# Late units of a gated-recurrence and SwiGLU kernel: packing transfers on another queue, a 16-bit step in the weight decoding, another order inside transposes, and decayed k turned without TensorE

## The chip, the cores and the metric

The kernel runs on one core of one Trainium2 chip. The metric is the device time in microseconds (us) of one execution. Three timed executions of the kernel before gave a median of 611.0 us (610.39 to 611.38). One further execution was profiled; all profile lines come from it.

## The reference

The first half is a linear recurrence with a gate, for 4 batches, 8 heads, 768 tokens and 48 dimensions per head. The second half is a feed-forward block with 384 model and 1536 hidden dimensions on all 3072 tokens.

```
f = sigmoid(f_logit)
for t in range(S):
    state = f[t][:, None] * state + outer(k[t], v[t])      # per batch and head, 48 x 48
    y[t] = q[t] @ state
x = y as (B*S, H*D)
out = (silu(x @ w_gate) * (x @ w_val)) @ w_out
```

q, k, v and f_logit are 32-bit floats. The three weight matrices arrive as 64-bit floats, so the kernel has to make 32-bit floats of them itself.

## The kernel before, in words

**Units and chunks.** Tokens are cut into six chunks of 128 (`c` = 0 to 5). A unit `u` is one batch `b` of one chunk, numbered chunk by chunk: u = 4c + b, 24 units in all. One run of the generator `attention(u)` (L529) is one unit. It yields between its steps, and these steps are placed between other work. Two heads share one 128-partition tile (64 partitions each, 48 of them used), so a unit has four such pairs of heads (`HP` = 4).

**The steps of a unit.** Sigmoid of f; f, k and q transposed so that tokens lie along the free dimension; a backward scan of the gates into `tail` (L576), whose first column `whole` is the decay over the entire chunk; k multiplied with `tail` (L584, "decayed k", tile `kT`); a forward scan into `gate` (L598); q multiplied with `gate` (L604, tile `qT`); scores `sc` on TensorE (L617) and their masking into `A` on VectorE (L631); the old state times `whole` (`decay`, L537); the output `y` on TensorE; the update `dS` of the state (L697), which needs decayed k with tokens on the partitions again (`kt`); the new state (L706). ScalarE copies `whole` into a column of `least` (L623), which is checked once near the end.

**Two routes for the transposes.** Units of chunks 0 and 1 transpose f, k and q on TensorE. Units of chunks 2 to 5 (`c >= SQUARES`) transpose on VectorE: f, k and q are loaded into three single rooms (`rooms`, L398) such that VectorE's transpose of 32 x 32 squares gives the wanted layout (L565, L572, L601). Token t of a chunk has four residues i = t mod 4; each square holds one residue, so its transpose writes with a step of four elements. The f, k and q of the next unit are loaded (`load_after`, L709) once q has been transposed.

**kt.** In units 0 to 13 TensorE transposes decayed k (four instructions, L621) into PSUM and ScalarE copies it out (L629). In units 14 to 19 (`turned`, L586) VectorE transposes squares of decayed k into the room of the coming `qT` (`beside`, L591), four DMAs on SP's queue write it to a DRAM tile `turn` (L594), and one DMA on SP's queue reads it back as `kt` (L627). The last chunk needs no kt.

**From y to the block.** For batches 0 to 2 of a chunk, ScalarE copies `y` from PSUM into `yT` (L660) and ten DMAs on SP's queue pack it into `xT[c]` (L667). For batch 3, `decay` also builds a tile `diagonal`: GpSimd clears it (L544), two ScalarE copies fill it (L546), TensorE uses it for y (L677), and ScalarE copies y straight into `xT[c]`. `yT` and `diagonal` are the same buffer (tag "x", one buffer), so clearing `diagonal` of batch 3 waits until the packing DMAs of batch 2 have read `yT`.

**The feed-forward block.** Chunk 0 is computed plainly (`mlp_plain`). Chunks 1 to 5 use `mlp_fifteen`: fifteen products in place of eighteen for gate and val, four times, and then seven products in place of eight for the way down (`down_seven`, L1033), in the order one, six, two, three, four, five, seven. After "two", ScalarE copies the PSUM tile out (L1082), after which product "four" may use that bank again. While chunk c is in its block, units of chunk c+1 run beside it. Results go out by DMA (L800, L1065).

**Weights.** Each weight piece is fetched, ScalarE makes two 32-bit words from the two halves of each 64-bit number (`sizes`, L458: `up` and `top`), and VectorE joins them (`join`, L466): a clamp (L469), a shift and mask (L471), the two top bits of the number put on with `scalar_tensor_tensor` (L473, one instruction for each of `b // parts` slices), and an exact addition (L475).

**What sets the order.** `in_order` (L724) chains the instructions of each engine, SP and GpSimd among them, in the order in which they were traced. In the late part (from L1253) that order comes from a list of due times written by hand (`SCORES`, `CHAINS`, L828 to L842) against a clock that counts TensorE's work. So an instruction that waits holds up everything traced after it on its engine.

Of the kernel before, what the change touches and what calls it, by code (L numbers as in the profile page):

```python
# [9 lines left out]
FP32 = mybir.dt.float32  # L10
I32 = mybir.dt.int32
U32 = mybir.dt.uint32
AF = mybir.ActivationFunctionType
ALU = mybir.AluOpType

# [274 lines left out]
def short_path(ctx, tc, ident, least, judge, q, k, v, f_logit, moe_w_gate, moe_w_val, moe_w_out, out):  # L290
# [9 lines left out]
    nc = tc.nc  # L300
    B, H, S, D = q.shape
    C = 128
    NCH = S // C
    HP = H // 2
# [6 lines left out]
    N1 = C + 1  # L311
# [3 lines left out]
    SQUARES = 2  # L315
# [47 lines left out]
    def pairs(t, off=0):  # L363
        return t[:, off:off + HP * N1].rearrange("p (a t) -> p a t", t=N1)
# [30 lines left out]
    NI = C // Q  # L395
    RUN = NI * D

    rooms = {}  # L398
# [6 lines left out]
    def v_of(u):  # L405
        return vs[u % (NV if units[u][1] < SQUARES else NV // 2)]

    def squares(nm):
        return rooms[nm][:, Q:Q + HP * RUN].rearrange("t (a i e) -> t a i e", a=HP, i=NI)[:, :, :, 0:Q]

    def in_turn(t):

        return t.rearrange("p a (t i) -> p a i t", i=NI)

    def load(u, what="fkqv"):
        b, c = units[u]
        rows = slice(c * C, (c + 1) * C)
        for nm, src in (("f", f_logit), ("k", k), ("q", q), ("v", v)):
            if nm not in what:
                continue  # L420
            if nm == "v":
                dst = v_of(u)
            elif c < SQUARES:
                dst = raw[nm][u % NRAW]
            else:
                for n in range(4):
                    at = Q * (1 - n % 2)
                    nc.sync.dma_start(
                        out=rooms[nm][Q * n:Q * (n + 1), at:at + HP * RUN].rearrange("t (a e) -> t a e", a=HP),
                        in_=src[b, n // 2::2, rows, :].rearrange("a (t i) d -> t a (i d)", i=NI))  # L430
                continue
            nc.sync.dma_start(out=dst[:, :, 0:D], in_=src[b, :, rows, :].rearrange("h t d -> t h d"))

    def weight_piece(dst, src, parts):

        b, a, n = dst.shape[1:]  # L440
        if src.dtype == FP32:
            by_row = src.rearrange("p a (b n) -> p a b n", n=n)
            return (lambda: [nc.sync.dma_start(out=dst[:, :, i], in_=by_row[:, i]) for i in range(a)]), [], []
        shape = [128, b // parts, a, n]
        kept = {}

        def fetch():
            kept["w"] = wst.tile([128, a, 2 * b * n], I32, tag="w64", name="w64", bufs=4)
            nc.sync.dma_start(out=kept["w"], in_=src)

        def part(m):
            return slice(m * b // parts, (m + 1) * b // parts)

        def halves(m):
            words = kept["w"].rearrange("p a (b n two) -> p a b n two", two=2, n=n)[:, :, part(m)].rearrange("p a b n two -> p b a n two")
            return words[:, :, :, :, 0], words[:, :, :, :, 1]

        def sizes(m):  # L458
            lo, hi = halves(m)
            up = wst.tile(shape, I32, tag="up", name="up", bufs=NPART)  # L460
            nc.scalar.activation(up, lo.bitcast(U32), AF.Copy, scale=2.0 ** -29)
            top = wst.tile(shape, I32, tag="top", name="top", bufs=NPART)
            nc.scalar.activation(top.bitcast(FP32), hi.bitcast(FP32), AF.Abs)
            kept["up", m], kept["top", m] = up, top

        def join(m):  # L466
            lo, hi = halves(m)
            up, top = kept["up", m], kept["top", m]
            nc.vector.tensor_scalar(top.bitcast(FP32), top.bitcast(FP32), as_float(0x38000000), as_float(0x47F00000),  # L469
                                    op0=ALU.max, op1=ALU.min)  # L470
            nc.vector.tensor_scalar(top, top, 3, 0x3FFFFFFF, op0=ALU.logical_shift_left, op1=ALU.bitwise_and)  # L471
            for i in range(b // parts):
                nc.vector.scalar_tensor_tensor(top[:, i], hi[:, i], -(1 << 30), top[:, i], op0=ALU.bitwise_and,  # L473
                                               op1=ALU.bitwise_or)
# [35 lines left out]
    xT = {}  # L510
# [18 lines left out]
    def attention(u):  # L529
        b, c = units[u]  # L530
        fr, kr, qr = (raw[nm][u % NRAW] for nm in "fkq")
        v_ = v_of(u)
        gate, tail = (x[u % NROT if c < SQUARES else 0] for x in (gates, tails))

        diagonal = None

        def decay():  # L537
            nonlocal diagonal
            if c:
                nc.vector.tensor_tensor(decayed[:, :, 0:D], states[b], whole.broadcast_to((128, HP, D)), ALU.mult)  # L540
            if c and b == B - 1:

                diagonal = att.tile([128, HP, 2 * D], FP32, tag="x", name="diagonal")
                nc.gpsimd.memset(diagonal, 0.0)  # L544
                for par in range(2):
                    nc.scalar.copy(diagonal[rows_of(par), :, par * D:(par + 1) * D], decayed[rows_of(par), :, 0:D])  # L546
# [13 lines left out]
        else:  # L560
            p = transposed("fTp", fr)
# [22 lines left out]
        nc.vector.tensor_tensor(kT, kp, pairs(tail, 2)[:, :, 0:C], ALU.mult)  # L584
        yield
        turned = (SQUARES + 1) * B + 1 < u < (NCH - 1) * B  # L586
        if turned:


            beside = qT.rearrange("p a t -> p (a t)").rearrange("p (i m) -> p i m", i=NI)  # L590
            nc.vector.transpose(beside.rearrange("p i (a e) -> p a i e", e=Q), kT.rearrange("p a (i e) -> p a i e", e=Q))  # L591
            turn = turn_pool.tile([Q, NI, HP, NI, Q], FP32, tag="turn", name="turn")
            for r in range(NI):
                nc.sync.dma_start(out=turn[:, :, :, r, :].rearrange("t i a e -> t (i a) e"),  # L594
                                  in_=beside[Q * r:Q * (r + 1)].rearrange("t i (a e) -> t (i a) e", e=Q))
        yield

        nc.vector.tensor_tensor_scan(gate[:, 0:n], gate[:, 0:n], start, 1.0, op0=ALU.mult, op1=ALU.add)  # L598
        yield
        if c >= SQUARES:  # L600
            nc.vector.transpose(in_turn(qT), squares("q"))  # L601
            load_after(u)
        yield
        nc.vector.tensor_tensor(qT, qp, pairs(gate)[:, :, 1:N1], ALU.mult)  # L604
        nc.gpsimd.memset(pairs(gate)[:, :, 0:1], 0.0)
        if 0 < c < SQUARES:
            load_after(u)
# [6 lines left out]
        for a in range(HP):  # L614
            for par in range(2):
                r = rows_of(par)
                nc.tensor.matmul(sc[par][:, a * C:(a + 1) * C], lhsT=kT[r, a, :], rhs=qT[r, a, :], start=True, stop=True)  # L617
        if c < NCH - 1 and not turned:
            p = bank("kt")
            for a in range(HP):  # L620
                nc.tensor.transpose(p[:, a * C:(a + 1) * C], kT[:, a, :], ident)  # L621
        yield
        nc.scalar.copy(least[:, u, :], whole.rearrange("p a t -> p (a t)"))  # L623
        if c < NCH - 1:
            kt = att.tile([128, HP * C], FP32, tag="kt", name="kt")
            if turned:
# [13 lines left out]
        if c and b < B - 1:  # L640
# [17 lines left out]
            yT = att.tile([128, 2, HP // 2 * C], FP32, tag="x", name="yT")  # L658
            for par in range(2):
                nc.scalar.copy(yT[:, par, :], y[par][:, 0:HP // 2 * C])  # L660
            for h in range(H):
                a, par = h // 2, h % 2
                f = h * D
                while f < (h + 1) * D:
                    n = min((h + 1) * D, (f // 128 + 1) * 128) - f
                    r = W * (a % 2) + f - h * D
                    nc.sync.dma_start(out=xT[c][f % 128:f % 128 + n, f // 128, b * C:(b + 1) * C],  # L667
                                      in_=yT[r:r + n, par, a // 2 * C:(a // 2 + 1) * C])
                    f += n
        else:  # L670

# [22 lines left out]
        if c < NCH - 1:  # L694
            p = bank("dS")
# [129 lines left out]
    whole = NJ * TRIPLE + 7 * DOWN  # L825
# [82 lines left out]
    def lag(f, *args):  # L908
        lagging.append(lambda: f(*args))  # L909
# [123 lines left out]
    def down_seven(c, h):  # L1033
# [7 lines left out]
        kept = {}  # L1041
# [321 lines left out]
```

## Time and profile before

| | |
|---|---|
| median of three executions | 611.0 us |
| the profiled execution | 611.44 us |
| its span, first to last instruction | 609.6 us |
| TensorE matmuls busy | 595.8 us |
| VectorE busy | 494.3 us |
| ScalarE busy | 288.5 us |
| GpSimd busy | 7.6 us, 52 instructions |
| DMA issues on SP's queue for packing (L667) | 150 |
| DMA issues on SP's queue for kt by way of DRAM (L594, L627) | 24 + 6 |

In a line of instruction groups the columns are: line, engine, operation, output and input tiles, shapes, count, then busy us in all, mean ns of one, and the idle time just before them with what ended it. In a timeline they are: start, duration (both us from the start of the span), engine, line, operation, tiles, count, and in brackets the idle time before and what ended it. SPq is SP's queue. Matmul ends are modelled, so starts are the safer reading.

### The profile page before, as it was taken

The numbers are of one execution on the slowest core, as the hardware profiler recorded it, in microseconds if no ns is written. First come the engines' busy times: TensorE is split into PE (matmuls) and PEld (weight loads), VectorE is DVE, ScalarE is ACT, GpSimd is POOL, SyncE is SP. The second block draws the span as 40 slices with busy tenths as digits, with TensorE's granted clock in tenths as the row PEclk, the third lists the DMA queues.
The fourth block names the chain that finished last, engine by engine and source line by source line (L and its number), as shares of the span: only waits on it lengthen the run. The fifth ranks groups of instructions, "written<-read, shape, count | busy, mean of one in ns | idle before, by whom it ended". The sixth has DMA issues, their size and how long they took to land.

```text
span 609.6 us, 10796 instructions
## 1 busy us (share of the span) xinstructions
PE 595.8 (98%) x4036; PEld 491.1 (81%) x4036; DVE 494.3 (81%) x833; ACT 288.5 (47%) x554; POOL 7.6 (1%) x52
## 2 busy tenths in 40 slices
PE   7899999999999999999999999999999999999996
PEld 5744545667888799888899988899988899988896
DVE  7999989868999985999996789996878981566731
ACT  3466644313776522476732366742276730366600
POOL 1000000000000000000000000000000000000000
PEclk9999999999999999999999999999999999999999
DMA  9988372005312044323236334145313100100001
GB/s 199 260 194 295 126 247 79 5 15 159 95 39 70 23 108 115 105 53 96 61 89 145 94 97 110 35 112 120 110 44 90 27 6 10 53 1 1 0 1 59
DMA packets 109142, 54.10 MB, mean 89 GB/s; under 512 B 68760, under 2 KB 102168, under 8 KB 109080
## 3 DMA queue, kind: packets, MB, share of 16 engines
q1 hardware_dynamic: 107064, 50.56, 31.3%
q10 hardware_dynamic: 2016, 2.75, 1.2%
q8 instruction: 34, 0.56, 0.4%
q14 instruction: 28, 0.23, 0.1%
HBM read 44.04 MB, written 6.29 MB: 83 GB/s over the span
## 4 chain that ended last, share of the span: by engine, by line
PE 85%; DVE 10%; SPq 1%; issue 1%; DMA 1%; ACT 1%; POOL 0%; DVEq 0%; ACTq 0%; POOLq 0%
PE o L1056 17%; PE A L957 15%; PE B L957 12%; PE gate L755 5%; PE val L755 5%; PE o L957 5%; PE c L957 5%; PE sc L617 4%; PE o L778 3%; PE o L1119 3%; PE y L677 2%; PE y L656 2%; PE dS L697 2%; PE y L652 1%; DVE c L861 1%
## 5 line engine op out<-in xcount | busy, mean ns | idle before, releaser
L1056 PE MATMUL o<-w_out,h 128*128 128x192 f32 x360 | 62.0, 327 | 0.5 <-DVE h L909 0.5
L957 PE MATMUL A<-xs,w_both 128*128 128x256 f32 x240 | 62.1, 381 | 0.0
L1056 PEld LDWEIGHTS o<-w_out,h 128*128 128x128 f32 x360 | 58.7, 190 | 1.7 <-DVE h L909 0.8
L962 ACT COPY c<-A 128x512 f32<-128x512 f32 x40 | 23.3, 583 | 62.6 <-PE A L957 62.6
L962 ACT COPY aside<-A 128x512 f32<-128x512 f32 x60 | 35.1, 584 | 32.6 <-PE A L957 32.6
L858 DVE TENSOR_TENSOR c<-c,aside 128x512 f32<-128x512 f32 x60 | 41.6, 694 | 10.5 <-ACT aside L962 9.0
L957 PEld LDWEIGHTS A<-xs,w_both 128*128 128x128 f32 x240 | 44.9, 190 | 6.5
L909 DVE TENSOR_TENSOR h<-h,c 128x256 f32<-128x256 f32 x100 | 41.1, 419 | 7.3 <-ACT h L973 7.3
L861 DVE TENSOR_TENSOR c<-c,aside 128x512 f32<-128x512 f32 x60 | 41.4, 689 | 2.5 <-ACT aside L962 2.5
L973 ACT ACTIVATE h<-c 128x256 f32<-128x256 f32 x100 | 39.2, 416 | 8.4 <-DVE c L858 5.8
L1056 PE MATMUL o<-ws,h 128*128 128x192 f32 x240 | 41.5, 328 | 0.2 <-DVE A L631 0.2
L957 PE MATMUL B<-xs,w_both 128*128 128x256 f32 x160 | 41.2, 380 | 0.6 <-ACT aside L962 0.6
L957 PE MATMUL c<-xT,w_both 128*128 128x256 f32 x160 | 41.2, 380 | 0.5 <-DVE c L861 0.5
L957 PE MATMUL A<-xs,extra 128*128 128x256 f32 x160 | 41.2, 380 | 0.0
L957 PE MATMUL B<-xT,extra 128*128 128x256 f32 x160 | 41.1, 379 | 0.0
L962 ACT COPY aside<-B 128x512 f32<-128x512 f32 x60 | 35.1, 584 | 11.7 <-PE B L957 7.2
L631 DVE TENSOR_TENSOR A<-sc,causal 128x512 f32<-128x512 f32 x48 | 30.8, 684 | 11.3 <-PE sc L617 11.3
L1056 PEld LDWEIGHTS o<-ws,h 128*128 128x128 f32 x240 | 39.1, 190 | 0.8 <-DVE A L631 0.4
L861 DVE TENSOR_TENSOR c<-o,c 128x512 f32<-128x512 f32 x40 | 27.6, 690 | 10.0 <-ACT h L973 5.8
L957 PEld LDWEIGHTS c<-xT,w_both 128*128 128x128 f32 x160 | 30.3, 190 | 5.0 <-DVE c L861 0.9
L957 PEld LDWEIGHTS B<-xs,w_both 128*128 128x128 f32 x160 | 30.2, 190 | 5.0 <-ACT aside L962 1.0
L957 PEld LDWEIGHTS A<-xs,extra 128*128 128x128 f32 x160 | 30.3, 190 | 4.5 <-ACT c L962 0.4
(138 smaller groups left out, 1140.2 us busy)
## 6 DMA issues: line engine op xcount, KB each, us to landing
fsquares<-in_f_logit_dram SPq DMA_DIRECT2D x64, 96.0 KB, 2.6
ksquares<-in_k_dram SPq DMA_DIRECT2D x64, 96.0 KB, 2.3
qsquares<-in_q_dram SPq DMA_DIRECT2D x64, 96.0 KB, 2.2
v<-in_v_dram SPq DMA_DIRECT2D x24, 192.0 KB, 3.0
w<-in_moe_w_gate_dram SPq DMA_DIRECT2D x6, 768.0 KB, 6.3
w<-in_moe_w_val_dram SPq DMA_DIRECT2D x6, 768.0 KB, 5.1
w<-in_moe_w_out_dram SPq DMA_DIRECT2D x6, 768.0 KB, 5.3
out_dram<-ob ACTq DMA_DIRECT2D x14, 192.0 KB, 2.7
```

The lines of the kernel that those rows point to most:

```text
L617: nc.tensor.matmul(sc[par][:, a * C:(a + 1) * C], lhsT=kT[r, a, :], rhs=qT[r, a, :], start=True, stop=True)
L631: nc.vector.tensor_tensor(A[:, par], sc[par].rearrange("p (a t) -> p a t", t=C), causal.unsqueeze(1).broadcast_to((128, HP, C)), ALU.mult)
L755: nc.tensor.matmul(p, lhsT=w[:, j, i, :], rhs=xT[c][:, i, :], start=(i == 0), stop=(i == KT - 1))
L778: nc.tensor.matmul(p, lhsT=hidden_tile(h, n // 2)[:, n % 2 * 2 + b // 2, b % 2 * C:(b % 2 + 1) * C], rhs=w_out[:, j, :], start=(n == 0), s ...
L858: nc.vector.tensor_tensor(dst, a, b, ALU.add)
L861: nc.vector.tensor_tensor(dst, a, b, ALU.subtract)
L909: lagging.append(lambda: f(*args))
L957: nc.tensor.matmul(p[name][:, n, :], lhsT=weights_of[a][:, n, j, :], rhs=tokens[b], start=fresh and n == 0, stop=True, skip_group_check=True)
L962: nc.scalar.copy(t, p[name])
L973: nc.scalar.activation(dst, src[:, 0, :], AF.Silu)
L1056: nc.tensor.matmul(p[:, n, :], lhsT=lhsTs[j][:, n * C:(n + 1) * C], rhs=rhs[:, j, :], start=first and j == order[0] and n == 0, stop=j == ...
L1119: nc.tensor.matmul(p, lhsT=hidden_tile(h, j)[:, 2, n * C:(n + 1) * C], rhs=b22[:, j, :], start=j == order[0], stop=j == order[-1])
```

## The change

- **Packing.** For chunks 2 to 5 the packing DMAs (L667, 120 of the 150) go to GpSimd's queue, and so do the two output DMAs of L1065 in every chunk but the last.
- **16-bit ops for the top bits.** ScalarE writes `up` as 16-bit numbers into the low half of each 32-bit word. VectorE then puts the two top bits into the high half, by one 16-bit instruction per piece that reads every fourth 16-bit number of the source and writes every second one. The `scalar_tensor_tensor` of L473 goes.
- **Pairs in transposes.** For k and q of chunks 2 to 5 the transpose writes with a step of two elements (two residues side by side, the other two in another half of the tile). The multiplication that follows (`multiply`) reads its operand in that order. k's transpose now goes to the room of `qT`, and q's to the room of `tail`; since that overwrites `whole`, the copy to `least` on ScalarE comes before the forward scan, and `whole` is read from `least` afterwards.
- **Decayed k by VectorE and DRAM.** `turned` holds for all twelve units of chunks 2 to 4 (u = 8 to 19), and `beside` lies in k's room.
- **Loads.** For chunks 2 to 5 q is loaded ahead of k.

```
-        for nm, src in (("f", f_logit), ("k", k), ("q", q), ("v", v)):
+        for nm in "fkqv" if c < SQUARES else "fqkv":
...
-            nc.scalar.activation(up, lo.bitcast(U32), AF.Copy, scale=2.0 ** -29)
+            ends = up.bitcast(U16).rearrange("p b a (n two) -> p b a n two", two=2)
+            nc.scalar.activation(ends[:, :, :, :, 0], lo.bitcast(U32), AF.Copy, scale=2.0 ** -29)
...
-            for i in range(b // parts):
-                nc.vector.scalar_tensor_tensor(top[:, i], hi[:, i], -(1 << 30), top[:, i], op0=ALU.bitwise_and,
-                                               op1=ALU.bitwise_or)
+            ends = up.bitcast(U16).rearrange("p b a (n two) -> p b a n two", two=2)
+            nc.vector.tensor_single_scalar(ends[:, :, :, :, 1], high_ends(m), 0xC000, op=ALU.bitwise_and)
             nc.vector.tensor_tensor(dst[:, part(m)].bitcast(I32), top, up, ALU.add)
...
+        def multiply(out, x, by):
+            if c >= SQUARES:
+                for_each = "p a (t j i) -> p a t j i"
+                out, by = (t.rearrange(for_each, j=2, i=NI // 2) for t in (out, by))
+                x = x.rearrange("p (j a t i) -> p a t j i", j=2, a=HP, i=NI // 2)
+            nc.vector.tensor_tensor(out, x, by, ALU.mult)
...
         if c >= SQUARES:
-            nc.vector.transpose(in_turn(kT), squares("k"))
+            kp = qT.rearrange("p a t -> p (a t)")
+            nc.vector.transpose(parted(kp), split_squares("k"))
...
-        turned = (SQUARES + 1) * B + 1 < u < (NCH - 1) * B
+        turned = SQUARES <= c < NCH - 1
         if turned:
-            beside = qT.rearrange("p a t -> p (a t)").rearrange("p (i m) -> p i m", i=NI)
+            beside = rooms["k"][:, 0:HP * C].rearrange("p (i m) -> p i m", i=NI)
...
+        if c >= SQUARES:
+            nc.scalar.copy(least[:, u, :], whole.rearrange("p a t -> p (a t)"))
+            whole = least[:, u, :].unsqueeze(2)
         nc.vector.tensor_tensor_scan(gate[:, 0:n], gate[:, 0:n], start, 1.0, op0=ALU.mult, op1=ALU.add)
         yield
         if c >= SQUARES:
-            nc.vector.transpose(in_turn(qT), squares("q"))
+            qp = tail[:, 0:HP * C]
+            nc.vector.transpose(parted(qp), split_squares("q"))
             load_after(u)
         yield
-        nc.vector.tensor_tensor(qT, qp, pairs(gate)[:, :, 1:N1], ALU.mult)
+        multiply(qT, qp, pairs(gate)[:, :, 1:N1])
...
-                    nc.sync.dma_start(out=xT[c][f % 128:f % 128 + n, f // 128, b * C:(b + 1) * C],
-                                      in_=yT[r:r + n, par, a // 2 * C:(a // 2 + 1) * C])
+                    (nc.gpsimd if c >= SQUARES else nc.sync).dma_start(out=xT[c][f % 128:f % 128 + n, f // 128, b * C:(b + 1) * C],
+                                                                       in_=yT[r:r + n, par, a // 2 * C:(a // 2 + 1) * C])
...
-            lag(put_out, 0, n, nc.sync)
+            lag(put_out, 0, n, nc.sync if c == NCH - 1 else nc.gpsimd)
```

More of the change, by code (lines that the diff above doesn't have):

```diff
@@ L12 @@
 U32 = mybir.dt.uint32
+U16 = mybir.dt.uint16
 AF = mybir.ActivationFunctionType
@@ L409, in squares, with split_squares, parted @@
         return rooms[nm][:, Q:Q + HP * RUN].rearrange("t (a i e) -> t a i e", a=HP, i=NI)[:, :, :, 0:Q]
+    def split_squares(nm):
+        return squares(nm).rearrange("t a (j i) e -> t a j i e", j=2)
     def in_turn(t):
         return t.rearrange("p a (t i) -> p a i t", i=NI)
+    def parted(t):
+        return t.rearrange("p (j a t i) -> p a j i t", j=2, a=HP, i=NI // 2)
     def load(u, what="fkqv"):
@@ L417, in load @@
         rows = slice(c * C, (c + 1) * C)
-        for nm, src in (("f", f_logit), ("k", k), ("q", q), ("v", v)):
+        inputs = dict(f=f_logit, k=k, q=q, v=v)
+        for nm in "fkqv" if c < SQUARES else "fqkv":
+            src = inputs[nm]
             if nm not in what:
@@ L456, in halves, with high_ends @@
             return words[:, :, :, :, 0], words[:, :, :, :, 1]
+        def high_ends(m):
+            quarters = kept["w"].bitcast(U16).rearrange("p a (b n four) -> p a b n four", four=4, n=n)[:, :, part(m)]
+            return quarters.rearrange("p a b n four -> p b a n four")[:, :, :, :, 3]
         def sizes(m):
@@ L583, in attention @@
             qp = transposed("qTp", qr)
-        nc.vector.tensor_tensor(kT, kp, pairs(tail, 2)[:, :, 0:C], ALU.mult)
+        multiply(kT, kp, pairs(tail, 2)[:, :, 0:C])
         yield
-        turned = (SQUARES + 1) * B + 1 < u < (NCH - 1) * B
+        turned = SQUARES <= c < NCH - 1
         if turned:
-            beside = qT.rearrange("p a t -> p (a t)").rearrange("p (i m) -> p i m", i=NI)
+            beside = rooms["k"][:, 0:HP * C].rearrange("p (i m) -> p i m", i=NI)
             nc.vector.transpose(beside.rearrange("p i (a e) -> p a i e", e=Q), kT.rearrange("p a (i e) -> p a i e", e=Q))
@@ L622, in attention @@
         yield
-        nc.scalar.copy(least[:, u, :], whole.rearrange("p a t -> p (a t)"))
+        if c < SQUARES:
+            nc.scalar.copy(least[:, u, :], whole.rearrange("p a t -> p (a t)"))
         if c < NCH - 1:
```

## The prediction

> **What bounds the kernel.** I read busy times first, then instruction groups, waits, and the timeline of the stretches where a wait reaches TensorE.
>
> ```profile
> PE 595.8 (98%) x4036; PEld 491.1 (81%) x4036; DVE 494.3 (81%) x833; ACT 288.5 (47%) x554; POOL 7.6 (1%) x52
> ...
> L621 PE MATMUL kt<-idf,kT 128*128 128x128 f32 x56 | 9.2, 287 | 0.0
> L601 DVE STREAM_TRANSPOSE qT<-qsquares 128x512 f32<-128x512 f32 x16 | 18.0, 1125 | 6.4 <-DMA turn<-qT 6.4
> L591 DVE STREAM_TRANSPOSE qT<-kT 128x512 f32<-128x512 f32 x6 | 4.2, 702 | 0.0
> L473 DVE SCALAR_TENSOR_TENSOR top<-w,top 128x384 int32<-128x384 int32 x24 | 12.6, 554 | 0.4
> L471 DVE TENSOR_SCALAR top<-top 128x768 int32<-128x768 int32 x16 | 8.9, 554 | 0.3
> ```
>
> TensorE is the bound: it works in 595.8 of 609.6 us. Only work taken from it, or a wait of its own, moves the time. The waits that reach it, and two that don't yet:
>
> ```profile
> PE sc L617 <- DVE qT L604: 2.5, 3, 1.0
> ...
> ACT diagonal L546 <- POOL diagonal L544: 40.8, 5, 8.9
> POOL diagonal L544 <- DMA xT<-yT: 38.5, 4, 13.0
> ```
>
> The last two are a chain: packing DMAs of batch 2, then GpSimd's clearing of `diagonal` (same buffer as `yT`), then ScalarE. In the timeline of chunk 5's units:
>
> ```profile
> 499.52 0.81 ACT L660 COPY yT<-y 128x256 f32<-128x256 f32 x2 [2.66 <-PE y L656]
> 499.92 6.21 SPq L667 DMA_DIRECT2D xT<-yT  x10
> 508.26 0.42 POOL L544 MEMSET diagonal<- 128x384 f32 x1 [8.76 <-DMA xT<-yT]
> 508.71 0.71 ACT L546 COPY diagonal<-decayed 48x192 f32<-48x192 f32 x2 [8.28 <-POOL diagonal L544]
> 509.44 0.48 ACT L1082 COPY ob<-o 128x384 f32<-128x384 f32 x1
> 510.79 4.06 PE L1056 MATMUL o<-ws,hs 128*128 128x192 f32 x24
> ```
>
> L1082 frees the bank that product "four" (last line) writes. It is queued on ScalarE behind the diagonal copies, and ends at 509.92, with 510.79 as TensorE's need: less the 0.06 of a handover, 0.81 us are spare. A longer packing goes straight to TensorE beyond that.
>
> **What the Trainium skill says.**
> - "DMA: Bandwidth & Descriptors", Specifications: first byte about 1 us for a GpSimd DMA, about 0.6 for one issued from SP. SP agrees (6.21 / 10 = 0.62 us each); no GpSimd DMA is in this trace.
> - "SBUF — State Buffer", Door 1 (the box on cachelines): full rate needs two accesses to each 16-byte line. The trace agrees: the step of 16 bytes costs 1125 ns (L601), the dense write 702 (L591). A step of 8 bytes isn't shown.
> - "VectorE: DVE Perf Modes", Mode 2×_2P: one-source operations within SBUF run two elements a cycle. L471 agrees: 768 elements in 554 ns, what the two-source L473 takes for 384.
> - "SBUF — State Buffer", Who interferes with whom: GpSimd can't write descriptors while VectorE is in such a mode. From 499.9 to 510 VectorE runs two-source operations only, so I add nothing.
>
> **Part by part.** Own time of the profiled execution 611.44, span 609.6; the median, 611.0, is 0.44 below it. The sum is a change to that execution.
>
> *Decayed k.* Six units (8 to 13) lose four transposes. The chain of waits has them at 0.59 us per unit (for example 225.08 to 225.68). But where no such group follows the scores, the next four matmuls take 1.06 instead of 0.86 us (at 292.79, against 247.47), so 0.39 net: 6 × 0.39 = −2.3 us on TensorE (−3.5 at most). ScalarE's six copies (L629, 585 ns) go too, in slack. Added: six VectorE transposes of 702 ns and 6 × 5 SP issues of about 0.62 us. The read waits for the four writes (3.1 us to land, 5.3 at worst). The tightest new unit is 11: decayed k at 219.2, writes issued to about 222.5, landed by 228 at worst, read landed by about 232, and dS starts at 238.28. So the latency is hidden; without that cover a late kt would stop TensorE by its lateness. k's load now waits for the writes, with the read and v queued behind it on SP; unit 12's k comes some 1.5 us later than the 227.93 at which it is transposed now, but its scores are due at 245.8. In return q's transpose no longer waits for the writes (6.4 us of VectorE idle, of which TensorE felt 0.15).
>
> *Pairs.* 32 transposes (k and q of 16 units). Bounds 702 and 1113 ns; I take 702 since pairs give two accesses per line: −13 us of VectorE. The multiplications (674 and 696 ns) read such pairs; bounds 0.67 and 1.1; I take no change. Less the 4.2 us above, VectorE gains 9 us, nearly all in slack. Where VectorE is behind (176 to 210 us), units 9 and 10 gain 4 × 0.41 and pay 2 × 0.70, so TensorE's 1.5 us of waits there stay. q's transpose newly waits for ScalarE's copy to `least`; TensorE's next scores would wait behind it only if ScalarE were blocked, which is the case costed below.
>
> *16-bit step.* 24 × 554 + 6 × 956 ns = 19.0 us become 16 instructions of 768 and 4 of 384 elements. At two per cycle (L471: 554 and 360) 10.3 us, at one per cycle (956 and 554) 17.5. I take the former: −8.7 us. From 109 to 126 us VectorE is behind, and the scores at 126.50 wait 0.78 us for qT. The one L473 inside that stretch (124.20, 0.95 us) saves 0.40, the shorter queue ahead of it may save the rest: −0.8 us (0 at worst). TensorE is full elsewhere before 145 us after its start-up.
>
> *Packing.* Let t be the time for which one DMA holds GpSimd's queue. Bounds: 0.6 (SP's) and 1.2 us (twice SP's); I take the page's 1.0. Ten in a row take 10t, landing as now (2.13 us from the last issue's end to the clearing). For chunks 3, 4, 5:
> - Chunk 5: 10.0 − 6.21 = 3.8 later, 0.81 spare: +3.0.
> - Chunk 4: SP takes 6.26; L1082 ends at 417.00, needed at 418.85, 1.79 spare: +1.9.
> - Chunk 3: SP takes 6.81; 323.32 against 324.87, 1.49 spare: +1.7.
> - Chunk 2: batch 1's packing starts at 213.11, so with t = 1.0 it lands at 225.24, and batch 2's `yT` (now 223.19) waits for it. First copy 0.4, ten DMAs, 2.13, clearing 0.45, first diagonal copy 0.4: TensorE's y (now 236.17) starts at 238.67, +2.5. It would be ready earlier by the two kt groups of units 10 and 11, and waits instead: +0.8 of the gain above is lost. Now SP starts 2.9 us late behind loads; that gain is in these numbers.
>
> Sum: +9.9 us. GpSimd's other work behind these DMAs, the clearing of `gates` (L605), is needed only some 10 us later. The moved output DMAs lie in slack. Late next behind the blocked ScalarE: nothing but L1082 and the `least` copy.
>
> *Sum.* −2.3 − 0.8 − 0.15 + 9.9 = +6.7 us: 611.44 + 6.7 − 0.44 = 617.7 us. Per 0.1 us of t: at 0.9 the loss is 4.9 (612.7), at 0.8 it is 0.5 (608.3), at 1.2 it is 19.9 (627.7). Break-even lies near t = 0.86.
>
> **Rivals.**
> 1. *GpSimd issues about as fast as SP.* With t from 0.6 to 0.8, L1082 keeps its slack, chunk 2's wait (0.48) goes, and the gains stand: 607.3 to 608.3, faster. For: the first-byte time needn't hold the queue. Against: the page's 1.0, and t must be below 0.86. This is the one that ends on the other side.
> 2. *Pairs don't pay.* Transposes stay at 1113 ns and multiplications take 1.1 us. In the stretch 176 to 210 that adds 4 × 0.43 + 2 × 0.70 = 3.1 us to a VectorE already behind, and TensorE pays: 620.8 with t = 1.0, about 611 with t = 0.8. For: no 8-byte writing step is in this trace. Against: L473 reads with a step of 8 bytes at one element a cycle.
> 3. *kt comes late.* DRAM round trips queue on SP behind loads; unit 11 has some 6 us of margin. At 2 us late in three units: 623.7. Against: SP sheds 120 issues of 0.62 us.
> 4. *A part without its effect.* 16-bit step at one element a cycle: 0.8 less, 618.5; it doesn't decide the sign.
>
> **How the numbers follow.** A difference under about 0.2% (1.2 us) can't be told from none. Chances: forecast with t of 0.9 to 1.2, 0.54; rival 1, 0.26; rival 2, 0.12; rival 3, 0.05; rival 4 and others, 0.03. Faster: rival 1 less a little, 0.25. Same: t near 0.86, and rival 2 at small t, 0.08. Slower: 0.67. Range: 607 (rival 1) to 627 (t near 1.2); the forecast's own range is 612.5 to 627.
>
> **What would show it.**
> - Ten packing issues on GpSimd's queue take 9 to 12 us; the wait of `diagonal` clearing on the DMAs rises from 38.5 to about 53 us; product "four" gets a wait on L1082 (2 to 3 us, three times) and chunk 2's y one on the diagonal copy. Ten issues in under 8 us prove rival 1.
> - L601 and L572 near 700 ns, L584 and L604 below 750; otherwise rival 2.
> - No L621 in units 8 to 13, and no wait of L697 on kt; otherwise rival 3.
> - 16-bit instructions at 554 ns, no wait of scores on qT at 126 us.
>
> I am wrong if TensorE's idle time after 200 us doesn't grow.

## The result, and the profile after

The changed kernel takes 613.28 us (median of 22 executions, 611.4 to 616.63), the kernel before 610.4 us beside it (609.15 to 612.42). The ratio is 1.0047, 95% interval 1.0036 to 1.0057: 2.9 us slower, less than half of the forecast 6.7. Its profiled execution took 613.17 us, with a span of 611.5.

Busy times of each engine, changed kernel:

```profile
PE 593.3 (97%) x4012; PEld 487.6 (80%) x4012; DVE 478.9 (78%) x829; ACT 288.3 (47%) x548; POOL 72.4 (12%) x180
```

TensorE is busy for 2.5 us less (forecast 2.3) and VectorE for 15.4 us less (forecast 17.7), and the span is longer all the same: TensorE's idle time grows from 13.8 to 18.2 us. Most of GpSimd's 72.4 us are DMA issues, which count as busy there.

Groups of instructions, changed kernel (the parts that the change prices):

```profile
L698 POOL DMA_DIRECT2D xT<-yT x120 | 60.0, 508 | 52.0 <-ACT yT L691 50.7 <-DMA xT<-yT 1.3
...
L597 DVE STREAM_TRANSPOSE qT<-ksquares 128x512 f32<-128x512 f32 x16 | 11.3, 704 | 3.9 <-DMA ksquares<-in_k_dram 3.9
L631 DVE STREAM_TRANSPOSE tails<-qsquares 128x512 f32<-128x512 f32 x16 | 11.2, 699 | 0.6 <-ACT least L625 0.6
L559 DVE TENSOR_TENSOR qT<-tails,gates 128x512 f32<-128x512 f32 x16 | 10.9, 684 | 0.1
...
L490 DVE TENSOR_SCALAR up<-w 128x768 uint16<-128x768 uint16 x16 | 9.7, 608 | 0.1
```

The first line answers the prediction's largest unknown. A packing DMA holds GpSimd's queue for 508 ns, not for 1.0 us, and not even for SP's 0.62. L597 and L631 are the transposes in pairs (704 and 699 ns, before 1113 and 1125), L559 the multiplication that reads pairs (684 ns, before 696), L490 the 16-bit instruction.

Waits by engine, changed kernel, those of TensorE that are new or longer, and the chain of `diagonal` (columns: who waits for whom, us in all, times, longest us):

```profile
PE A L988 <- ACT c L993: 2.2, 2, 1.9
...
PE B L988 <- ACT aside L993: 1.1, 1, 1.1
PE o L1087 <- ACT ob L1113: 1.0, 1, 1.0
PE o L1087 <- DVE A L662: 0.8, 1, 0.8
```
```profile
ACT diagonal L570 <- POOL diagonal L568: 38.4, 5, 10.8
...
POOL diagonal L568 <- DMA xT<-yT: 14.0, 5, 5.5
```

Product "four" (third line of the first fence) waits once, for 1.0 us, where the forecast had three waits of 1.7 to 3.0. The largest new wait is in the first line: TensorE waits for a PSUM copy of ScalarE, 1.9 us at once, in a place that the prediction doesn't mention. It lies in the first unit that is newly turned (timeline of the changed kernel, 151 to 168 us, ScalarE, SP's queue and TensorE):

```profile
152.21 3.74 SPq L619 DMA_DIRECT2D turn<-ksquares  x4
156.04 2.00 SPq L440 DMA_DIRECT2D fsquares<-in_f_logit_dram  x4
...
160.51 1.28 ACT L580 ACT_TABLE_LOAD   x1 [3.53 <-DMA fsquares<-in_f_logit_dram]
161.80 0.63 ACT L580 ACTIVATE fsquares<-fsquares 128x512 f32<-128x512 f32 x1
162.34 0.57 ACT L993 COPY c<-A 128x512 f32<-128x512 f32 x1
...
162.96 1.13 PE L988 MATMUL A<-xs,w_both 128*128 128x256 f32 x4 [1.87 <-ACT c L993]
163.92 1.65 PE L988 MATMUL B<-xT,extra 128*128 128x256 f32 x4
165.36 1.91 PE L988 MATMUL o<-xs,extra 128*128 128x256 f32 x4
```

To be read from the top: the four writes of decayed k wait on SP's queue until VectorE has made `beside`; f of the next unit is queued behind them and goes out at 156.04, in the kernel before at 146.81; ScalarE stands for 3.53 us at the sigmoid of that f; the PSUM copy L993 is queued behind the sigmoid; TensorE needs the bank that it frees. Then four matmuls that take 1.03 us elsewhere take 1.65 and 1.91. The table by stretches of the changed kernel says why (columns: stretch and its length, busy time and count of PE, PEld, DVE, ACT and POOL, granted TensorE clock, DMA share, GB/s):

```profile
160.00:163.00 3.00, 1.13 (x7) 0.66 (x5) 0.48 (x1) 2.48 (x4) 0.00 (x0) 1.00 0.78 211
163.00:166.00 3.00, 3.00 (x10) 2.52 (x11) 3.00 (x6) 2.90 (x5) 0.00 (x0) 0.70 0.27 87
166.00:169.00 3.00, 3.00 (x11) 2.49 (x11) 2.96 (x6) 1.62 (x6) 0.00 (x0) 0.73 0.05 18
```

After the gap the mean granted clock of the next two stretches is 0.70 and 0.73. Asked more finely, it is 0.50 from 164.19 to 167.60 us and 1.00 on both sides. Over the work that the kernel before does from 159.8 to 173 us, TensorE falls back by 4.1 us: 1.9 by the wait, most of the rest by the clock.

In chunk 5 the packing went (timeline of the changed kernel; the lines of before are in the prediction):

```profile
500.25 0.81 ACT L691 COPY yT<-y 128x256 f32<-128x256 f32 x2 [2.67 <-PE y L687]
500.92 4.98 POOL L698 DMA_DIRECT2D xT<-yT  x10 [1.08 <-ACT yT L691]
...
507.31 0.42 POOL L568 MEMSET diagonal<- 128x384 f32 x1 [1.42 <-DMA xT<-yT]
```

From the start of the first `yT` copy to the clearing it takes 7.06 us, before 8.74. In chunk 4 the same ten DMAs do worse:

```profile
406.61 0.81 ACT L691 COPY yT<-y 128x256 f32<-128x256 f32 x2 [0.72 <-PE y L687]
407.27 4.98 POOL L698 DMA_DIRECT2D xT<-yT  x10 [1.08 <-ACT yT L691]
...
407.49 0.39 SPq L444 DMA_DIRECT2D v<-in_v_dram  x1
...
408.75 1.76 SPq L440 DMA_DIRECT2D fsquares<-in_f_logit_dram  x4
...
417.75 0.42 POOL L568 MEMSET diagonal<- 128x384 f32 x1 [5.50 <-DMA xT<-yT]
418.20 0.71 ACT L570 COPY diagonal<-decayed 48x192 f32<-48x192 f32 x2 [10.79 <-POOL diagonal L568]
...
418.94 0.48 ACT L1113 COPY ob<-o 128x384 f32<-128x384 f32 x1
...
419.47 4.17 PE L1087 MATMUL o<-ws,hs 128*128 128x192 f32 x24 [0.98 <-ACT ob L1113]
```

The same place in the kernel before:

```profile
407.13 0.81 ACT L660 COPY yT<-y 128x256 f32<-128x256 f32 x2 [0.72 <-PE y L656]
...
407.52 6.26 SPq L667 DMA_DIRECT2D xT<-yT  x10
...
413.89 0.53 SPq L432 DMA_DIRECT2D v<-in_v_dram  x1
...
415.33 0.42 POOL L544 MEMSET diagonal<- 128x384 f32 x1 [8.23 <-DMA xT<-yT]
```

In the changed kernel 11.14 us lie between the copy and the clearing, before 8.20. The issuing is as short as in chunk 5; the landing is what differs, 5.50 us against 1.42. In the stretch 406 to 412 us the DMA share is 0.77 (before 0.25): with packing gone from SP's queue, SP sends v, kt and f out at the same moment, which it used to send after the packing. In 500 to 506 us, without loads, the share is 0.09.

### The profile page after: what moved, and what is told of

Same layout as the page of the kernel before. It is cut to its first block, busy times and chain, and to the rows that moved or that the text cites. A ratio compares the mean times of both kernels' runs of the same rounds, so it can differ in the third digit from the quotient of the medians.

```text
span 611.5 us, 10807 instructions
## 1 busy us (share of the span) xinstructions
PE 593.3 (97%) x4012; PEld 487.6 (80%) x4012; DVE 478.9 (78%) x829; ACT 288.3 (47%) x548; POOL 72.4 (12%) x180
## 4 chain that ended last, share of the span: by engine, by line
PE 83%; DVE 11%; issue 2%; DMA 1%; ACT 1%; POOL 1%; SPq 0%; DVEq 0%; POOLq 0%; ACTq 0%
PE o L1087 17%; PE A L988 15%; PE B L988 12%; PE gate L786 5%; PE val L786 5%; PE c L988 5%; PE o L988 5%; PE sc L647 4%; PE o L1150 3%; PE o L809 3%; PE y L687 2%; PE y L708 2%; PE dS L728 2%; DVE c L892 1%; PE y L683 1%
## 5 line engine op out<-in xcount | busy, mean ns | idle before, releaser
L698 POOL DMA_DIRECT2D xT<-yT x120 | 60.0, 508 | 52.0 <-ACT yT L691 50.7
L993 ACT COPY aside<-A 128x512 f32<-128x512 f32 x60 | 35.1, 585 | 33.2 <-PE A L988 33.2
L889 DVE TENSOR_TENSOR c<-c,aside 128x512 f32<-128x512 f32 x60 | 41.0, 684 | 11.6 <-ACT aside L993 9.9
L993 ACT COPY c<-A 128x512 f32<-128x512 f32 x40 | 23.3, 583 | 56.8 <-PE A L988 56.8
L662 DVE TENSOR_TENSOR A<-sc,causal 128x512 f32<-128x512 f32 x48 | 30.8, 683 | 16.2 <-PE sc L647 16.1
L635 POOL MEMSET gates<- 128x4 f32 x24 | 3.0, 123 | 321.2 <-DVE qT L559 316.1
L993 ACT COPY aside<-B 128x512 f32<-128x512 f32 x60 | 35.1, 585 | 10.7 <-PE B L988 6.9
L889 DVE TENSOR_TENSOR c<-c,o 128x384 f32<-128x384 f32 x15 | 8.2, 549 | 34.7 <-PE o L1087 34.7
```

What stands on the lines that cost most here:

```text
L662: nc.vector.tensor_tensor(A[:, par], sc[par].rearrange("p (a t) -> p a t", t=C), causal.unsqueeze(1).broadcast_to((128, HP, C)), ALU.mult)
L698: (nc.gpsimd if c >= SQUARES else nc.sync).dma_start(out=xT[c][f % 128:f % 128 + n, f // 128, b * C:(b + 1) * C], in_=yT[r:r + n, par, a / ...
L889: nc.vector.tensor_tensor(dst, a, b, ALU.add)
L993: nc.scalar.copy(t, p[name])
```

## The experiments

A ratio is to the kernel before on the same chip (610.4 to 610.6 us); where two other kernels are compared, their medians are. Two theories stood at the start. **Theory N** (new): the loss is f's load behind the writes of decayed k, as just read. **Theory P** (predicted): the loss is packing on GpSimd's queue.

**1. f ahead of the writes.** The changed kernel, with f of the next unit loaded before this unit's writes of decayed k (f's room is free by then), k and q as before.

```
+        if c >= SQUARES:
+            load_after(u, "f")
         if turned:
...
-            load_after(u)
+            load_after(u, "kq")
```

> The changed kernel, with f of the next unit loaded just before the writes of decayed k to DRAM instead of behind them on SP's queue. Theory N (f's load sits behind these writes, and ScalarE's sigmoid, waiting for f, holds up its PSUM copies): ScalarE's wait for f near 160 us (3.5 us in the changed kernel) and TensorE's wait there (1.87 us, and a lower clock for 6 us after it) are gone; time 4 us under the changed kernel, about 609.3 us, a little under the kernel before. Theory P (the packing on GpSimd's queue is the loss): no difference, 613.3 us within 0.7.

Measured: 610.57 us, ratio 1.0001 (0.9989 to 1.0013). 2.7 of the 2.9 us are gone, and f's lateness is confirmed as the largest single loss. It isn't all: theory N's 609.3 would have been faster than before. The waits of TensorE in this run:

```profile
PE o L1089 <- ACT ob L1115: 1.6, 2, 1.0
PE B L990 <- ACT aside L995: 1.1, 1, 1.1
PE c L990 <- ACT c L995: 0.9, 1, 0.9
```

The wait of 1.9 us is gone. The first line is the packing's landing, in chunks 4 and 3; the wait in chunk 3 (0.62 us) is not in the changed kernel, so it seems to come with this run's edit. The other two lines come back below.

**2. Packing back on SP's queue**, all else as in the changed kernel.

```
-                    (nc.gpsimd if c >= SQUARES else nc.sync).dma_start(out=xT[c]...
+                    nc.sync.dma_start(out=xT[c]...
...
-            lag(put_out, 0, n, nc.sync if c == NCH - 1 else nc.gpsimd)
+            lag(put_out, 0, n, nc.sync)
```

> The changed kernel, with the packing and the output DMAs back on SP's queue. Theory P: 4 us or more under the changed kernel, 609 us or less. Theory N: within 1.5 us of the changed kernel's 613.3, since GpSimd holds its queue for 0.50 us per DMA, less than SP's 0.62; the 1 us wait of chunk 4 goes, and loads wait behind packing again.

Measured: 620.47 us, ratio 1.0166 (1.0143 to 1.0189). Both theories missed, in the same direction: GpSimd's queue doesn't cost the changed kernel anything like the forecast, it saves it 7.2 us. Timelines of SP's queue and of TensorE in this run:

```profile
214.49 7.32 SPq L698 DMA_DIRECT2D xT<-yT  x10
221.90 0.54 SPq L444 DMA_DIRECT2D v<-in_v_dram  x1
222.49 0.61 SPq L658 DMA_DIRECT2D kt<-turn  x1
```
```profile
228.32 0.67 PE L728 MATMUL dS<-v,kt 128*64 128x48 f32 x16 [3.79 <-DMA kt<-turn]
```

The read of kt goes out only after ten packing DMAs, and dS waits 3.79 us for it. This is the third rival of the prediction, in a kernel where SP did not shed its 120 issues.

**3. Packing on GpSimd alone**, in the kernel before.

```
-                    nc.sync.dma_start(out=xT[c]...
+                    (nc.gpsimd if c >= SQUARES else nc.sync).dma_start(out=xT[c]...
...
-            lag(put_out, 0, n, nc.sync)
+            lag(put_out, 0, n, nc.sync if c == NCH - 1 else nc.gpsimd)
```

> The kernel before, with only the packing and the output DMAs moved to GpSimd's queue. Theory P (1.0 us per DMA, as predicted): plus 9.9 us, 620 us. Theory N: 609.9 to 611.5 us against 610.4, ten issues in 5 us, and at most a 1 us wait of one product for the copy behind the diagonal tile.

Measured: 612.35 us, ratio 1.0031 (1.0016 to 1.0046). So alone it does cost 1.9 us, a fifth of the forecast 9.9. Product "four" in chunk 4 waits 1.60 us for L1082 in that run, and nowhere else.

**4. Six turned units**, as in the kernel before; all else as in the changed kernel.

```
-        turned = SQUARES <= c < NCH - 1
+        turned = (SQUARES + 1) * B + 1 < u < (NCH - 1) * B
```

> The changed kernel, with decayed k by DRAM for units 14 to 19 only, as before; units 8 to 13 use TensorE and PSUM again. Theory N: the 4 us at 160 us go, six groups of transposes come back (2.3 us): 611.3 to 612 us. Theory P: only the transposes come back, 615.6 us.

Measured: 609.36 us, ratio 0.9982 (0.9973 to 0.999). Without the six more turned units the rest of the change is 1.1 us faster than before, and the six cost 3.9 us. That is more than f's 2.7, although they take 2.3 us off TensorE.

**5. Twelve turned units alone**, in the kernel before (`turned` and `beside` as changed, q loaded ahead of k, packing on SP).

```
-        turned = (SQUARES + 1) * B + 1 < u < (NCH - 1) * B
+        turned = SQUARES <= c < NCH - 1
...
-            beside = qT.rearrange("p a t -> p (a t)").rearrange("p (i m) -> p i m", i=NI)
+            beside = rooms["k"][:, 0:HP * C].rearrange("p (i m) -> p i m", i=NI)
```

> The kernel before with one part of the change alone: twelve turned units (with k's room for the squares and q loaded ahead of k); packing stays on SP's queue. Theory additive: the six more turned units cost the same wherever packing is issued, 613.3 less 609.4 = +3.9 us (f late in the first of them), so 614.4. Theory shared queue: with packing on SP too the round trip by DRAM comes late for dS on top of it, as when packing was put back on SP in the changed kernel (+7.2 us): 617 to 621, with waits of dS on kt.

Measured: 626.55 us, ratio 1.024 (1.0216 to 1.0264): 16 us, above even the dearer expectation. TensorE's waits in this run:

```profile
PE dS L699 <- DMA kt<-turn: 5.2, 2, 3.3
...
PE A L959 <- ACT c L964: 3.4, 2, 1.7
...
PE c L959 <- ACT c L964: 2.1, 1, 2.1
```

kt is late twice and f at the sigmoid as in the changed kernel. The parts are not additive: turning twelve units costs 16 us with packing on SP and long transposes, and 4 us with packing elsewhere and pairs.

**6. The 16-bit step alone**, in the kernel before (with `ends` and `high_ends` as in the change).

```
-            nc.scalar.activation(up, lo.bitcast(U32), AF.Copy, scale=2.0 ** -29)
+            nc.scalar.activation(ends[:, :, :, :, 0], lo.bitcast(U32), AF.Copy, scale=2.0 ** -29)
...
-                nc.vector.scalar_tensor_tensor(top[:, i], hi[:, i], -(1 << 30), top[:, i], op0=ALU.bitwise_and,
-                                               op1=ALU.bitwise_or)
+            nc.vector.tensor_single_scalar(ends[:, :, :, :, 1], high_ends(m), 0xC000, op=ALU.bitwise_and)
```

> The kernel before with the 16-bit step alone. Theory as predicted: VectorE is behind from 109 to 126 us, so the shorter join takes the scores' wait of 0.78 us near 126 us: 609.6 to 609.9, and nothing elsewhere. Rival: pairs made that gain, and the 16-bit step alone is in slack: 610.3 to 610.7.

Measured: 610.39 us, ratio 0.9996 (0.9986 to 1.0005). In the median no gain can be told from none; the forecast 0.8 lies at the edge of the interval. In the trace the wait of the scores at 126 us is 0.27 us, where it is 0.78 in the kernel before.

**7. Six turned units, packing on SP**, the edits of runs 2 and 4 in the changed kernel: what is left of the change is the 16-bit step, pairs and the load order.

```
-        turned = SQUARES <= c < NCH - 1
+        turned = (SQUARES + 1) * B + 1 < u < (NCH - 1) * B
...
+                    nc.sync.dma_start(out=xT[c]...
```

> The changed kernel with six turned units and with packing back on SP's queue: what is left of the change is the 16-bit step, pairs and the load order. Theory additive: packing on GpSimd costs 1.9 us here as it does alone in the kernel before, so 607.5. Rival: with pairs the loads and transposes sit otherwise, and packing on GpSimd costs nothing or helps: 609.4 or more.

Measured: 609.56 us, ratio 0.9982 (0.9974 to 0.9991). The rival holds: next to run 4 (609.36) packing on GpSimd costs nothing that can be told here, unlike in run 3. Yet run 4's trace has the wait of product "four" in chunk 4 (1.0 us) and this run's has none, so either packing on GpSimd also gains something in run 4, or the difference hides in the two intervals; which, is open. Pairs, the load order and the 16-bit step together gain 1.1 us.

**8. Packing divided**: six turned units, batches 0 and 1 packed on GpSimd's queue, batch 2, which the clearing of `diagonal` waits for, on SP's.

```
-                    (nc.gpsimd if c >= SQUARES else nc.sync).dma_start(out=xT[c]...
+                    (nc.gpsimd if c >= SQUARES and b < B - 2 else nc.sync).dma_start(out=xT[c]...
```

> The changed kernel with six turned units, with packing of batches 0 and 1 on GpSimd's queue and that of batch 2, which the clearing of diagonal waits for, on SP's. Theory landing: what packing on GpSimd costs is the landing of batch 2's ten DMAs beside loads; then this stands at 607.3 to 608.0, and product four has no wait over 1 us on the copy ahead of it. Rival: the cost is elsewhere (issue order, GpSimd's other work): 609.0 to 609.6.

Measured: 608.25 us, ratio 0.9958 (0.9945 to 0.9971), the fastest kernel of the study, 2.4 us below the kernel before; the theory expected up to 608.0. Its chunk 4:

```profile
405.81 6.26 SPq L698 DMA_DIRECT2D xT<-yT  x10
...
413.91 0.42 POOL L568 MEMSET diagonal<- 128x384 f32 x1 [9.96 <-DMA kt<-turn]
...
415.09 0.48 ACT L1113 COPY ob<-o 128x384 f32<-128x384 f32 x1
...
416.08 4.06 PE L1087 MATMUL o<-ws,hs 128*128 128x192 f32 x24
```

The issuing is longer (6.26 against 4.98 us), the clearing follows 1.84 us after its end (5.50 in the changed kernel), and product "four" doesn't wait. v, kt and f stand behind the packing on SP's queue, and so disturb its landing less. (The profile names the read of kt, issued at 412.75, as what released the clearing; so 1.84 us is the most that the packing's landing took.) This run changes the queue as well as the neighbours of batch 2's transfers; that the queue alone is not the cost is seen in chunk 5 of the changed kernel, where they land in 1.42 us from GpSimd's.

In the four kernels that pack chunks 2 to 5 on both queues (runs 8, 10, 11 and 12) each execution lasts 2.1 to 2.5 us longer than its span, in all others 1.7 to 1.9 us. So some 0.4 us of what this run gains within the span is lost outside it; no trace shows by what.

**9. VectorE's share.** Run 1, with f early, still stands 1.2 us above run 4 with its six turned units. Here six units are turned, and in units 8 to 13 VectorE makes the transposed decayed k too, but no DMA takes it: kt comes from TensorE as before.

```
-        if turned:
+        if turned or SQUARES <= c < NCH - 1:
             beside = ...
             nc.vector.transpose(beside..., kT...)
-            for r in range(NI):
+            for r in range(NI if turned else 0):
```

> The changed kernel with six turned units, and in units 8 to 13 VectorE also transposes decayed k into k's room, as the change has it, but no DMA takes it from there: kt is still made by TensorE, and that copy is never read. Theory VectorE: from 157 to 195 us VectorE runs without a gap, ScalarE's copies and TensorE wait for it, so 0.7 us more per unit there comes out at TensorE in about three of six units: 609.4 + 1.5 to 2.5 = 610.9 to 611.9. Rival DMA: what the six more turned units cost is transfers alone (f late, landing); VectorE has slack: 609.1 to 609.8.

Measured: 610.98 us, ratio 1.0012 (1.0004 to 1.002); over run 4 that is 1.6 us, for six instructions of 0.71 us. Timelines of this run, VectorE, ScalarE and TensorE:

```profile
186.84 0.71 DVE L616 STREAM_TRANSPOSE ksquares<-kT 128x512 f32<-128x512 f32 x1
...
190.16 0.68 DVE L889 TENSOR_TENSOR c<-c,aside 128x512 f32<-128x512 f32 x1
```
```profile
190.94 0.59 ACT L993 COPY aside<-B 128x512 f32<-128x512 f32 x1 [2.41 <-DVE c L889]
```
```profile
191.58 1.13 PE L988 MATMUL B<-xs,w_both 128*128 128x256 f32 x4 [1.00 <-ACT aside L993]
```

ScalarE's copy needs a buffer that L889 frees, VectorE comes to L889 only after the added transpose, and TensorE waits 1.00 us. In run 4 TensorE has no such wait in this place. From 150 to 260 us VectorE waits for no DMA in this run, so a load that comes later doesn't explain it. The wait is the second line of waits of run 1, and the second of the changed kernel.

**10. f ahead and packing divided**, with twelve turned units: the edits of runs 1 and 8 in the changed kernel.

```
+            load_after(u, "f")
...
+                    (nc.gpsimd if c >= SQUARES and b < B - 2 else nc.sync).dma_start(out=xT[c]...
```

> Twelve turned units, f of the next unit loaded before the writes of decayed k, and packing of batch 2 on SP's queue. Theory VectorE: only the landing wait of 1.6 us before product four goes, the waits behind VectorE at 169 and 191 us stay: 609.0 to 609.8. Rival DMA: with f early and batch 2's landing short nothing is left against the six more turned units, and the 2.3 us taken from TensorE show: 606.0 to 607.5. If batch 2's packing holds up the turned writes of unit 11 on SP's queue, a wait of dS on kt appears and it is 611 or more.

Measured: 613.25 us, ratio 1.0048 (1.0033 to 1.0063): the case that was named last. TensorE:

```profile
238.59 0.67 PE L730 MATMUL dS<-v,kt 128*64 128x48 f32 x16 [2.19 <-DMA kt<-turn]
```

It is the read of kt, not the writes, that goes out behind the ten packing DMAs (at 232.16 us; run 11 shows the same).

**11. Nine turned units** (11 to 19), otherwise as run 10, f ahead in the turned units only.

```
-        turned = SQUARES <= c < NCH - 1
+        turned = (SQUARES + 1) * B - 2 < u < (NCH - 1) * B
```

> Nine turned units (11 to 19), with f of the next unit ahead of their writes, and packing of batch 2 on SP's queue. Units 11 to 13 lie after the stretch in which VectorE is behind. Theory VectorE: three groups of transposes leave TensorE (3 x 0.39 = 1.2 us) at no price: 608.25 - 1.2 = 606.8 to 607.3. Rival DMA: each further turned unit costs by its transfers wherever it lies: 608.2 or more.

Measured: 611.85 us, ratio 1.0029 (1.0017 to 1.0042). The waits behind VectorE are gone, but dS of unit 11 waits 2.06 us for kt. SP's queue in this run:

```profile
223.35 6.90 SPq L700 DMA_DIRECT2D xT<-yT  x10
230.35 0.52 SPq L444 DMA_DIRECT2D v<-in_v_dram  x1
230.92 0.68 SPq L660 DMA_DIRECT2D kt<-turn  x1
```

In run 1, with all packing on GpSimd, that read of kt went out at 224.86.

**12. Eight turned units** (12 to 19), otherwise as run 11.

```
-        turned = (SQUARES + 1) * B - 2 < u < (NCH - 1) * B
+        turned = (SQUARES + 1) * B <= u < (NCH - 1) * B
```

> Eight turned units (12 to 19), otherwise as the run with nine. Theory queue: what the ninth, unit 11, cost was its read of kt, issued at 230.92 behind the ten packing issues of batch 2 on SP's queue (224.0 to 230.3); units 12 and 13 have no such packing ahead of their read, so the wait of dS on kt goes, and two groups of transposes leave TensorE: 608.25 - 2 x 0.39 = 607.2 to 607.8. Rival: each further turned unit costs wherever it lies: 608.3 or more.

Measured: 608.57 us, ratio 0.9972 (0.9963 to 0.9981). The wait on kt is gone, so the queue was the cost of the ninth unit. But the two units bring nothing: the interval overlaps with that of run 8. Against run 8, TensorE is 0.8 us further ahead at 289 us (the two groups, as worked out) and 0.8 us behind at 498 us, part of it by waits of 0.6 and 0.3 us on ScalarE's copies. Which of the two differences, the more turned units or f's earlier load in units 12 to 19, brings those is open.

## Why the prediction was right or wrong

The sign was right and the sum wrong, and the sign was right by luck, for another reason than the one given: the part that was to lose 9.9 us lost nothing in the changed kernel, and the part that was to gain 2.3 lost 3.9.

**Packing, +9.9.** The failed term is t, the time for which one DMA holds GpSimd's queue. The Trainium skill's page "DMA: Bandwidth & Descriptors" (Specifications) states a first byte after about 1 us, and the prediction took that for the hold; measured is 0.50 us, below its lower bound of 0.6, which was a copy of SP's figure. To compare it with SP's 0.62 us from issue to issue was the same mistake. What a page gives as the time to the first byte says nothing of how long the queue is held. "Landing as now" (2.13 us) failed too, the other way: 1.42 us without loads beside it, 5.50 with them. The mechanism itself (diagonal, then L1082, then product "four") showed once, for 1.0 us, in chunk 4. In sum packing on GpSimd costs 1.9 us alone (run 3), nothing that can be told beside pairs with six turned units (runs 4 and 7), and saves 7.2 us with twelve (run 2). The first rival, with t of 0.6 to 0.8, was nearest on this part (t is 0.5), but the whole came out slower, not faster.

**Decayed k, −2.3.** The four transposes are gone from all six units. The failed step is "So the latency is hidden": it followed what waits for kt, and of what SP has queued behind the turned writes only k's load. f's load is queued there as well, ahead of k's; behind f stand a sigmoid, a PSUM copy and TensorE. That cost 2.7 us (run 1). Two more terms were booked too low. VectorE's six transposes cost 1.6 us by themselves (run 9): two of them, at 166.1 and 186.8 us, lie in the stretch from 157 to 195 us, where VectorE is busy for 35.5 of 38 us even in run 4. The offset of 4 × 0.41 against 2 × 0.70 counted VectorE's total, and that total was not what TensorE waits for. And TensorE can't use all that it is spared. The starts of the scores show it:

| scores start at, us | unit 8 | unit 10 | unit 14 | unit 23 |
|---|---|---|---|---|
| run 4, six turned | 157.26 | 210.51 | 289.05 | 497.83 |
| run 9, the same and VectorE's six transposes | 156.64 | 211.13 | 289.67 | 498.60 |
| run 1, twelve turned, f early | 156.28 | 210.69 | 288.17 | 497.90 |

From unit 8 to unit 10 run 4 takes 53.25 us, run 9 54.49, and run 1, which lacks two groups of transposes (2 × 0.39 forecast), 54.41: these two groups gain next to nothing where VectorE is behind. From unit 10 to unit 14 run 1 gains 1.1 us on both, about three times 0.39 and not four times. The fourth group, unit 11's, had filled TensorE's wait for the masking: that wait is 0.78 us in run 1 and in the changed kernel (its line of waits on `A` L662 above), 0.19 in run 4. After unit 14 run 1 loses 0.9 us on run 4; the wait of 0.62 us for the packing in chunk 3 is in it. So 1.2 − 1.1 + 0.9 = 1.0 of the 1.2 us by which run 1's median stands above run 4's is seen, and with f's 2.7 it makes 3.7 of the 3.9 us. The figures come from one trace of each kernel.

**Pairs.** Right: 699 and 704 ns where 702 was taken, multiplications unchanged, so the second rival is out. This agrees with the Trainium skill, "SBUF — State Buffer" (Door 1): two accesses to each 16-byte line restore the full rate. That "nearly all" lies in slack held as well: 1.1 us is the gain of pairs, load order and 16-bit step together. Pairs were not run alone.

**16-bit step, −0.8.** Instructions of 608 ns instead of 554, so 12.0 us in place of the forecast 10.3 (and of 19.0). The wait of the scores at 126 us is 0.78 us in the three traces without the step (the kernel before, runs 3 and 5) and 0.27 to 0.28 in all those with it, run 6 among them. So half a microsecond of the 0.8 is there; it is too small to be told in run 6's median.

**Third rival.** kt is not late in the changed kernel, because packing has left SP. Put it back and dS waits 3.79 us. The prediction's reason against the rival was the right one.

**What would show it.** Of the four tests, "ten issues in under 8 us prove rival 1" came out at 4.98, no kt was late, and L601's and L572's successors were near 700 ns; the 16-bit instructions took 608 ns, not 554, and the scores still wait 0.27 us. The wait of the clearing on the DMAs fell to 14.0 us instead of rising to 53, since GpSimd now spends that time issuing: that sign could not be read any more. The closing condition, that TensorE's idle time after 200 us must grow, was met (from 6.6 to 9.3 us), but packing accounts for only 1.0 us of it, and so the condition could not tell the prediction's cause from another. The decisive place was before it: TensorE is 2.4 us ahead of the kernel before at 159.8 us and 1.6 us behind at 173. Of the lead some 1.4 us are not the change's: in the profiled execution of the kernel before the granted clock is 0.50 from 28.0 to 31.4 us, in those of the changed kernel and of run 3, which changes nothing so early, it is 1.00. The fall of 4.1 us is free of that.

## What to carry to other kernels

When a waiting DMA is put on a queue, list everything that is queued behind it, in the order of the changed code, and follow each to its reader and to what stands behind that reader. An engine that sets the pace in one stretch pays in full for what is moved onto it there, however much slack its total shows, and the engine that was relieved only waits longer. Moving transfers to a second queue also removes the spacing that the first queue gave them: they may then land together, so keep on the same queue, behind it, what should not overlap with the one transfer that is waited for, unless that too is waited for soon (runs 10 and 11).

## What the runs showed of the hardware that was not expected

- A packing DMA (8 to 24 KB) holds GpSimd's queue for 0.50 us (120 of them, 508 ns in the mean), SP's for about 0.62 (10 in 6.21 us). The first issue starts a little later: in chunk 5, 0.67 us after the start of the `yT` copies, on SP's queue 0.40.
- The landing of the same ten transfers, counted from the last issue to the clearing that waits for them, goes from 1.42 us (DMA share 0.09) to 5.50 us (share 0.77 at their issue).
- The Trainium skill's page "TensorE: Matmul & The Clock Gate" (What's actually happening) has the clock fall after an idle window of about 3.4 us. In these runs shorter gaps were enough at times: after 1.87 us of waiting the granted clock is 0.50 for 3.41 us, from 164.19 us on (changed kernel), and after dS had waited 2.06 us in run 11 it is 0.76 and 0.82 in two stretches of 4 us. But it stays at 1.00 after waits of 0.91 and 1.06 us (run 1), and also after 1.85 us (run 2, at 245.4 us) and 2.19 us (run 10, at 236.4 us). So a wait of TensorE near 2 us can cost about twice its length here, and need not; its length alone doesn't decide it, and what does is not shown.
